# A planner that books time on TensorE for each change of product kind, with ranks and leanings chosen anew

## Chip, cores and metric

One core of a Trainium2 chip runs the whole program in one launch. The metric is device microseconds (us) of one execution; several executions are made and their median is given. The profile is of one further execution of its own.

## What is computed

The reference runs three layers after one another on float32 data (the weights of the two feed-forward layers are float64): an attention in random features, a gated feed-forward layer, and a second one with a piecewise quadratic activation.

```python
def _attn_ref(q, k, v, omega):             # 4 batches, 8 heads, 576 rows, 64 columns; omega 128 x 64
    def phi(x):
        proj = np.einsum('bhsd,md->bhsm', x, omega)
        h = proj - np.sum(x * x, axis=-1, keepdims=True) / 2.0
        h = h - np.max(h, axis=-1, keepdims=True)
        return np.exp(h) / np.sqrt(m)
    q_p, k_p = (phi(q_s), phi(k_s))
    kv = np.einsum('bhsm,bhsd->bhmd', k_p, v)
    num = np.einsum('bhsm,bhmd->bhsd', q_p, kv)
    return num / (np.einsum('bhsm,bhm->bhs', q_p, np.sum(k_p, axis=2))[..., None] + 1e-06)

def _moe_ref(x, w_gate, w_val, w_out):     # 2304 tokens, 512 -> 1536 -> 512
    g = x @ w_gate
    return g / (1.0 + np.exp(-g)) * (x @ w_val) @ w_out

def _moe2_ref(x, w_in, w_out):             # 2304 tokens, 512 -> 2048 -> 512
    h = x @ w_in
    return np.where(h >= 1, h, np.where(h <= -1, 0.0, (h + 1) ** 2 / 4)) @ w_out
```

## The kernel before

**A planner writes the order.** The kernel is a set of Python generators that yield operations (`Op`: engine, cost in us, the function that issues it), requests for buffers (`Get`) and events (`Ev`). The class `Planner` runs them in a reckoned time while the program is built; whenever it starts an operation on an engine, that instruction is issued to this engine's queue. So the planner's reckoning fixes the order of every queue (TensorE, VectorE, ScalarE, GpSimd, and SyncE for the DMAs) and, through `pick` (L264), which engine does a copy or an addition that two engines can do. On the chip each engine then goes through its queue in that order and waits where its data is not there. The costs in the plan have no other effect on the program.

**How an engine chooses.** `dispatch` (L235) takes, of what is ready for an engine, the entry with the lowest rank (`PR_...`, L62 to L67; most processes without a rank of their own have 1.0). For TensorE, `together` (L223) first narrows the list: products have kinds. `row` is a projection on omega (L654, 64x128 tiles of the array), `col` are the sums over keys (L723) and the numerators (L836; both 128x64 tiles), `turn` are transposes by the identity (L792, L846; 128x128), and `moe`, or no kind, are the feed-forward products (L418 to L420; 128x128). While feed-forward products run, attention's products are held until two of them wait or one has waited 2.0 us (`HOLD`, `HOLD_N`); after that all ready ones of one kind go first, then those of another, before the feed-forward products go on. Such a stretch of attention's products between feed-forward products is called a visit here.

**What `pick` compares.** For each engine the time at which it is free, plus the costs that wait for it, plus the operation's cost, plus `LEAN` of this engine. `LEAN["DVE"]` (VectorE) is `LEAN_A` until attention is closed and `LEAN_B` from then on (L297, L903), and `LEAN["POOL"]` (GpSimd) becomes `POOL_B` at that point. `copy` (L396) chooses between ScalarE (0.52 us for 512 elements by the planner's formula) and VectorE (0.34 from SBUF, 0.60 from PSUM); `two` (L406) between VectorE (0.60) and GpSimd (1.23). `parts` makes the two halves of a number for the three products of `split3`: a copy (the high half, L399 or L401) and a subtraction (the low half, L409 or L411).

**The stages.** Until about 50 us TensorE has attention's products alone. From there to 230 us they alternate with the first part of the first feed-forward layer (`moe1`, nine token blocks of 256, weights of the first four column groups). From 230 us on all products are feed-forward ones: `late_up`, with sets of seven products over sums and differences of blocks (`set_up`, L1343), and `late_down`. `x_make` (L1157) makes the operands of these sets on VectorE and ScalarE, `stage` and `conv_pair` convert the float64 weights on the way (`PR_ST`, `PR_W`), `front` (L634) is the first half of attention for one group of rows (`PR_FRONT` is its rank after it has its banks), and `keep_bank` (L1249) copies a PSUM bank to SBUF (`PR_BANK`).

Of the kernel before, what the change touches and what calls it, by code (L numbers as in the profile page):

```python
# [35 lines left out]
KD = 4  # L36


LEAN = {'DVE': 1.0, 'POOL': -0.38, 'ACT': -0.55}
LEAN_A, LEAN_B, POOL_B = 0.97, -0.09, 5.00  # L40
ALT = 1.63

SLACK_D, SLACK_U = 2.0, 0.8
# [15 lines left out]
N_WT, N_XU = 3, 2  # L59
N_EB, N_GB, N_HL, N_HB, N_XI = 4, 2, 2, 1, 4  # L60

PR_K, PR_Q0, PR_Q = (0.32, 0.9, 0.96, 1.0), 0.17, 1.01  # L62
PR_C0, PR_C, PR_CS = 0.66, 1.08, 0.7
PR_W = 1.06
PR_BANK = 0.3
PR_FRONT = 0.2
PR_ST, PR_X, PR_E = 1.50, 0.74, 1.45  # L67
T_V, T_Q0, T_C0 = 3.84, 2.87, 5.5
N_GATE, N_CS = 1, 3
N_WS = 2  # L70
HOLD, HOLD_N = 2.0, 2

ORDER = (0, 1, 2, 3, 4)

SETS1 = (2, 2)
SETS2 = (2, 2)
# [58 lines left out]
class Planner:  # L135
# [99 lines left out]
    def dispatch(self, eng):  # L235
        q = self.queue.get(eng)
        if not q or self.free_at.get(eng, 0.0) > self.now + 1e-9:
            return
        held = self.port > self.now + 0.02
        c = self.together(q) if eng == "PE" else q  # L240
        best = q[0] if eng in ("HW", "DMA") else min(c, key=lambda e: (held and e[2].lock, e[1].prio, e[0]))
        if held and best[2].lock:
            self.push(self.port, self.dispatch, eng)
            return
        q.remove(best)
        _, p, op = best
        self.load[eng] -= op.cost
        if op.fn is not None:
            op.fn()
        end = self.now + op.cost  # L250
        if op.lock:
            self.port = end
        if eng == "PE":
            self.kind = op.kind
            if self.now > self.free_at.get(eng, 0.0) + 0.05:
                end += 0.12
            if self.now < 4.2:
                end += op.cost
        self.free_at[eng] = end
        p.last = {eng: end}  # L260
        self.push(end, self.step, p, None)
        self.push(end + (0.001 if op.kind == "moe" else 0.0), self.dispatch, eng)

    def pick(self, **cost):  # L264

        return min(cost, key=lambda e: max(self.now, self.free_at.get(e, 0.0)) + self.load.get(e, 0.0) + cost[e]
                   + LEAN.get(e, 0.0))

# [24 lines left out]
def performer_moe_kernel(ctx: ExitStack, tc: tile.TileContext, qX, kX, vX, om, ident,  # L293
                         w1, wo1, w2, wo2, out):
    nc = tc.nc
    pl = Planner()
    LEAN["DVE"] = LEAN_A  # L297
    scale = 64.0 ** -0.25
# [298 lines left out]
    def bank_pair():  # L597

        tok = yield Get(two_banks)
        b0 = yield Get(bank)  # L600
        b1 = yield Get(bank)
        pl.put(two_banks, tok)
        return b0, b1
# [30 lines left out]
    def front(xb, n, loads, is_q, rng):  # L634
# [13 lines left out]
        rank = pl.cur.rank  # L648
        pl.cur.rank = min(pl.cur.prio, PR_FRONT)

# [169 lines left out]
    def num(k, d, q_t):  # L820
# [8 lines left out]
        banks = yield from bank_pair()  # L829
        pl.cur.rank = min(pl.cur.prio, PR_FRONT)  # L830

# [54 lines left out]
    def att_close():  # L886
# [15 lines left out]
        pl.set(right_b)  # L902
        LEAN["DVE"], LEAN["POOL"] = LEAN_B, POOL_B  # L903

# [117 lines left out]
    def part_stream():  # L1022
        yield moe1_v
        for a in range(len(SETS1)):
            for kb in ORDER:
                nt = blocks[kb][1]
# [82 lines left out]
    for m, counts, sets in ((1, SETS1, list(range(NE, NF // 2))),  # L1109
                            (2, SETS2, [(2 * q, 2 * q + 1) for q in range(NF2 // 4)])):  # L1110
        for a, n in enumerate(counts):
            passes.append((m, a, ORDER, sets[0:n]))
            sets = sets[n:]
# [16 lines left out]
    def pq(t):  # L1130
        return t.rearrange("p (k t) -> p k t", k=2)
# [114 lines left out]
    def plus(dst, ps, e):  # L1246

        yield Op("DVE", c_dve(512), lambda: nc.vector.tensor_tensor(out=dst, in0=pq(ps), in1=pq(e), op=ALU.add))  # L1248

    def keep_bank(ps, ev, into):  # L1250
        e = yield Get(ebr)
        yield from copy(e, ps, 512, False)
        into.append(e)
        pl.set(ev)
# [40 lines left out]
    def row1(key, S):  # L1295
# [4 lines left out]
        cv = pq(c22)  # L1300
        pl.cur.rank = PR_BANK
        yield from plus(cv, S["Ub"], c22)
# [40 lines left out]
    def set_up(m, a, j, c, last_s, last_x):  # L1343
# [6 lines left out]
        for bk, wk, off, u, before, then in SEVEN:  # L1350
# [24 lines left out]
            if then in ("e1", "e2", "e5"):  # L1375
                pl.spawn(keep_bank(ps, S[then], S[then + "b"]), PR_BANK)
            else:
# [77 lines left out]
    def part2_stream():  # L1455
        for a in range(len(SETS2) - 1):
            for j in ORDER:
                for c in range(blocks[j][1] // P):
# [217 lines left out]
```

## Time and profile before

| | |
|---|---|
| median of 3 runs | 929.09 us (927.48 to 931.4) |
| the profiled execution | 930.79 us |
| its span, first to last instruction | 929.0 us |
| mean granted TensorE clock | 0.999 of full speed |
| busy: TensorE, VectorE, ScalarE, GpSimd | 920.5, 774.2, 512.6, 62.4 us |

An engine is busy while one of its instructions runs. A record of a matrix product includes its way through the array (276 ns for 256 columns), while the next one starts 113 ns later; so what TensorE loses is read from the starts of its products, and from the stretches in which nothing ran.

### The profile page before, as it was taken

Reading aid. Unit: us, or ns where it says so; the run is one execution under the profiler, and the core shown is the slowest. Engines: PE = TensorE matmul, PEld = TensorE weight load, DVE = VectorE, ACT = ScalarE, POOL = GpSimd, SP = SyncE. Lnnn points to the kernel's source line nnn. Section 1 sums busy time; section 2 is a strip of 40 time slices with the busy share of each in tenths; the row PEclk is TensorE's granted clock in tenths of the full one; section 3 lists DMA queues with packets and bytes.
Section 4 is the critical chain, followed back from the end, with each engine's and each line's share of the span. In section 5 each row is a group of like instructions: output and inputs, shape, how many; then the busy total and the mean of one; then the engine's idle time right before and its main releaser. Section 6 shows DMA issues by size and latency. Waiting matters only on the chain.

```text
span 929.0 us, 22669 instructions
## 1 busy us (share of the span) xinstructions
PE 920.5 (99%) x9244; PEld 906.6 (98%) x9244; DVE 774.2 (83%) x1496; ACT 512.6 (55%) x1131; POOL 62.4 (7%) x53
## 2 busy tenths in 40 slices
PE   8999999999999999999999999999999999999998
PEld 8889999999999999999999999999999999999998
DVE  5988888865989999899989899999797679766553
ACT  7888977544445545555545466555555445434331
POOL 0213324322000000000000000000000000000000
PEclk9999999999999999999999999999999999999999
DMA  7678446555676374845476836264313131403022
GB/s 247 192 237 252 143 160 217 198 180 167 222 233 193 112 235 167 308 146 187 137 240 208 267 113 213 80 211 153 126 58 125 37 112 47 137 12 103 1 92 91
DMA packets 88665, 147.71 MB, mean 159 GB/s; under 512 B 8304, under 2 KB 43888, under 8 KB 88560
## 3 DMA queue, kind: packets, MB, share of 16 engines
q1 hardware_dynamic: 88416, 146.19, 48.3%
q8 instruction: 72, 1.18, 0.5%
q14 instruction: 33, 0.27, 0.1%
q10 hardware_dynamic: 144, 0.07, 0.0%
HBM read 103.24 MB, written 42.99 MB: 157 GB/s over the span
## 4 chain that ended last, share of the span: by engine, by line
PE 83%; DVE 7%; DMA 6%; ACT 2%; issue 1%; SPq 0%; DVEq 0%; ACTq 0%
PE bank L418 25%; PE bank L419 25%; PE bank L420 25%; PE bank L654 4%; PE bank L723 2%; PE bank L836 2%; PE bank L792 1%; DMA ws<-in_w_dram 1%; DMA ki<-in_kX_dram 1%; DMA wtr<-w32i 1%; PE bank L846 1%; DMA ws<-in_wo_dram 1%; DVE xq L411 1%; DMA wtr<-w32o 1%; DMA kl<-in_kX_dram 1%
## 5 line engine op out<-in xcount | busy, mean ns | idle before, releaser
L418 PE MATMUL bank<-x1s,w 128*128 128x256 f32 x492 | 138.0, 280 | 0.2
L420 PE MATMUL bank<-x1s,w 128*128 128x256 f32 x492 | 136.2, 277 | 0.0
L419 PE MATMUL bank<-x1s,w 128*128 128x256 f32 x492 | 136.2, 277 | 0.0
L418 PEld LDWEIGHTS bank<-x1s,w 128*128 128x128 f32 x492 | 92.5, 188 | 1.5 <-ACT qt L399 0.3
L420 PEld LDWEIGHTS bank<-x1s,w 128*128 128x128 f32 x492 | 92.5, 188 | 0.0
L419 PEld LDWEIGHTS bank<-x1s,w 128*128 128x128 f32 x492 | 92.4, 188 | 0.0
L399 ACT ACTIVATE x1s<-xq 128x512 fp32r<-128x512 f32 x84 | 52.9, 631 | 60.7 <-PE bank L420 37.8
L418 PE MATMUL bank<-x1s,wb 128*128 128x256 f32 x286 | 78.9, 276 | 0.0
L419 PE MATMUL bank<-x1s,wb 128*128 128x256 f32 x286 | 78.9, 276 | 0.0
L420 PE MATMUL bank<-x1s,wb 128*128 128x256 f32 x286 | 78.9, 276 | 0.0
L418 PE MATMUL bank<-x1s,wx 128*128 128x256 f32 x278 | 77.4, 278 | 0.4 <-ACT eb L399 0.4
L419 PE MATMUL bank<-x1s,wx 128*128 128x256 f32 x278 | 76.8, 276 | 0.0
L420 PE MATMUL bank<-x1s,wx 128*128 128x256 f32 x278 | 76.8, 276 | 0.0
L435 ACT ACTIVATE wt<-ws 128x512 f32<-128x512 f32 x68 | 46.3, 684 | 46.7 <-DMA ws<-in_w_dram 23.4
L399 ACT ACTIVATE eb<-bank 128x512 f32<-128x512 f32 x96 | 56.6, 590 | 25.4 <-PE bank L420 25.1
L411 DVE TENSOR_TENSOR x1s<-xq,x1s 128x512 fp32r<-128x512 f32 x90 | 62.4, 694 | 7.5 <-ACT x1s L399 7.4
L663 DVE TENSOR_REDUCE st<-bank 128x4 f32<-128x512 f32 (+1 forms) x76 | 48.0, 659 | 17.1 <-PE bank L654 17.0
L1248 DVE TENSOR_TENSOR gb<-bank,eb 128x512 f32<-128x512 f32 x64 | 44.4, 693 | 12.7 <-PE bank L420 12.5
L419 PEld LDWEIGHTS bank<-x1s,wb 128*128 128x128 f32 x286 | 53.7, 188 | 0.0
L420 PEld LDWEIGHTS bank<-x1s,wb 128*128 128x128 f32 x286 | 53.7, 188 | 0.0
L418 PEld LDWEIGHTS bank<-x1s,wb 128*128 128x128 f32 x286 | 53.7, 188 | 0.0
L418 PEld LDWEIGHTS bank<-x1s,wx 128*128 128x128 f32 x278 | 52.2, 188 | 1.1 <-ACT eb L399 0.6
(253 smaller groups left out, 3322.6 us busy)
## 6 DMA issues: line engine op xcount, KB each, us to landing
ws<-in_w_dram SPq DMA_DIRECT2D x40, 512.0 KB, 4.7
ws<-in_wo_dram SPq DMA_DIRECT2D x28, 512.0 KB, 5.3
xq<-x1d SPq DMA_DIRECT2D x36, 256.0 KB, 4.7
xq<-x2d SPq DMA_DIRECT2D x36, 256.0 KB, 4.0
qi<-in_qX_dram SPq DMA_DIRECT2D x28, 256.0 KB, 4.2
ki<-in_kX_dram SPq DMA_DIRECT2D x22, 256.0 KB, 4.7
x1d<-os SPq DMA_DIRECT2D x18, 256.0 KB, 4.7
op<-os SPq DMA_DIRECT2D x18, 256.0 KB, 2.8
```

What stands on the lines that cost most here:

```text
L399: yield Op("ACT", c_act(n), lambda: nc.scalar.activation(dst, src, AF.Copy, scale=1.0 if scale is None else scale))
L411: yield Op("DVE", c_dve(n), lambda: nc.vector.tensor_tensor(out=dst, in0=a, in1=b, op=op), True)
L418: nc.tensor.matmul(ps, l_hi, r_hi, start=first, stop=False, skip_group_check=shared)
L419: nc.tensor.matmul(ps, l_hi, r_lo, start=False, stop=False, skip_group_check=shared)
L420: nc.tensor.matmul(ps, l_lo, r_hi, start=False, stop=last, skip_group_check=shared)
L435: yield Op("ACT", 0.575, lambda: nc.scalar.activation(t, hw.bitcast(F32), AF.Abs))
L654: nc.tensor.matmul(banks[a][:, u * P:(u + 1) * P], xb[h, l, u * P:(u + 1) * P], r[h], start=first and (last or u == 0), stop=last, skip_gr ...
L663: yield Op("DVE", c_dve(256 * n), lambda: nc.vector.tensor_reduce(out=sv[:, a, units, 3 if by_pe else 0], in_=pv[a], axis=AX.X, op=ALU.max ...
L723: nc.tensor.matmul(kp[h, 2 * pr + a, 0:65], es[:, a, u * P + 64 * m:u * P + 64 * m + 64], v[:, 65 * a:65 * a + 65], start=(li == 0 and a = ...
L792: nc.tensor.transpose(tp[:, (a * 2 + t) * P:(a * 2 + t + 1) * P], es[:, a, u * P:(u + 1) * P], ids)
L836: nc.tensor.matmul(banks[t][rows, 65 * h:65 * h + 65], q_t[:, h // 2, h % 2, t * P + 64 * m:t * P + 64 * m + 64], kvr[tiles[t][m], d][:, h ...
L1248: yield Op("DVE", c_dve(512), lambda: nc.vector.tensor_tensor(out=dst, in0=pq(ps), in1=pq(e), op=ALU.add))
```

## The change

The class `Planner` gets a table `SWITCH`, and `dispatch` adds time to a TensorE operation that is not of the kind of the one before it: nothing from `turn` to a feed-forward product or to no kind, 0.12 us from these to `turn`, 0.2 us for every other change; from `moe` to no kind and back nothing. Besides, some of the leanings and ranks have new values. No process, buffer or instruction of the kernel is edited.

```diff
-LEAN = {'DVE': 1.0, 'POOL': -0.38, 'ACT': -0.55}
-LEAN_A, LEAN_B, POOL_B = 0.97, -0.09, 5.00
+LEAN = {'DVE': 1.0, 'POOL': -0.586, 'ACT': -0.322}
+LEAN_A, LEAN_B, POOL_B = 0.823, -0.524, 5.0
...
-PR_K, PR_Q0, PR_Q = (0.32, 0.9, 0.96, 1.0), 0.17, 1.01
-PR_C0, PR_C, PR_CS = 0.66, 1.08, 0.7
+PR_K, PR_Q0, PR_Q = (0.32, 0.9, 0.96, 1.082), 0.17, 1.129
+PR_C0, PR_C, PR_CS = 0.68, 1.234, 0.7
 PR_W = 1.06
-PR_BANK = 0.3
-PR_FRONT = 0.2
-PR_ST, PR_X, PR_E = 1.50, 0.74, 1.45
+PR_BANK = 0.194
+PR_FRONT = 0.33
+PR_ST, PR_X, PR_E = 1.5, 0.491, 1.45
...
+SWITCH = {("turn", "moe"): 0.0, ("turn", None): 0.0, ("moe", "turn"): 0.12, (None, "turn"): 0.12}
...
         if eng == "PE":
+            if op.kind != self.kind and not (self.kind in ("moe", None) and op.kind in ("moe", None)):
+                end += SWITCH.get((self.kind, op.kind), 0.2)
             self.kind = op.kind
```

## Rows read from the trace of the kernel before

**Rows 1.** The page: busy time of each engine, and the granted clock by slices.

```profile
PE 920.5 (99%) x9244; PEld 906.6 (98%) x9244; DVE 774.2 (83%) x1496; ACT 512.6 (55%) x1131; POOL 62.4 (7%) x53
...
PEclk9999999999999999999999999999999999999999
```

**Rows 2.** Stages: stretch, length, busy us (instructions) by engine, clock, DMA share, GB/s.

```profile
12.00:54.00 42.00, 40.64 (x770) 37.00 (x766) 39.13 (x81) 37.23 (x111) 9.13 (x7) 1.00 0.71 226
54.00:230.00 176.00, 175.27 (x2255) 167.69 (x2254) 140.66 (x323) 121.58 (x374) 51.51 (x39) 1.00 0.58 188
230.00:300.00 70.00, 70.00 (x614) 69.61 (x613) 63.22 (x119) 36.37 (x65) 1.29 (x1) 1.00 0.68 224
300.00:650.00 350.00, 348.88 (x3066) 347.88 (x3066) 334.32 (x634) 189.85 (x354) 0.00 (x0) 1.00 0.57 184
650.00:925.00 275.00, 275.00 (x2429) 275.00 (x2429) 193.16 (x336) 120.68 (x215) 0.00 (x0) 1.00 0.24 78
```

**Rows 3.** TensorE's waits, whole span: waiting line, releaser, total us, times, longest.

```profile
PE bank L418 <- ACT eb L399: 1.0, 2, 0.6
PE bank L846 <- DVE os L401: 0.7, 1, 0.7
...
PE bank L654 <- ACT os L399: 0.7, 1, 0.7
```

**Rows 4.** The chain that ended last, its end: start, length, engine, line.

```profile
925.26 0.13 PE bank L420
...
925.41 0.42 DVE os L1512
```

**Rows 5.** TensorE's timeline around three visits (start, length, line, tiles, count).

```profile
72.66 0.28 PE L420 MATMUL bank<-x1s,w 128*128 128x256 f32 x1
72.87 1.16 PE L654 MATMUL bank<-omr,ki 64*128 64x128 f32 x16
73.96 0.38 PE L418 MATMUL bank<-x1s,w 128*128 128x256 f32 x1
...
112.57 0.28 PE L420 MATMUL bank<-x1s,w 128*128 128x256 f32 x1
112.69 1.04 PE L792 MATMUL bank<-ids,ebq 128*128 128x128 f32 x8
113.48 0.36 PE L418 MATMUL bank<-x1s,wx 128*128 128x256 f32 x1
...
222.59 0.28 PE L420 MATMUL bank<-hl,w 128*128 128x256 f32 x1
222.80 2.09 PE L836 MATMUL bank<-kvr,qt 128*64 128x65 f32 x64
224.82 0.38 PE L418 MATMUL bank<-hl,w 128*128 128x256 f32 x1
```

**Rows 6.** The chain in the first 230 us: pieces of one kind, short and long.

```profile
18.91 1.09 PE bank L654 x16
20.00 0.59 PE bank L792 x4
31.86 1.99 PE bank L654 x32
33.84 1.08 PE bank L836 x32
...
156.34 2.02 PE bank L836 x64
```

**Rows 7.** Copies, 300 to 650 us: L399 on ScalarE, L401 on VectorE; one form of L401.

```profile
300.00:650.00 350.00, 127.44 (x223) 1.00 0.57 184
300.00:650.00 350.00, 5.12 (x12) 1.00 0.57 184
L401 DVE CAST xur<-xq x7: 418/427/430, 322.2 to 826.6; 128x512 fp32r<-128x512 f32 x7
```

**Rows 8.** GpSimd's subtraction L409, its first 230 us (shortest/median/longest ns).

```profile
L409 POOL TENSOR_TENSOR x1s<-os,x1s x14: 1282/1346/1882, 42.6 to 212.3; 128x512 fp32r<-128x512 f32 x14
```

## Prediction, made before the changed kernel was run

> **What bounds the kernel now.** The page comes first. TensorE is busy for 920.5 of 929.0 us, and its granted clock is at the upper of its two levels (2.4 GHz) in every slice [rows 1], so neither more clock nor a large hole is to be had. The table by stages says where the missing 8.5 us lie: 1.36 between 12 and 54 us, 0.73 between 54 and 230, nothing from 230 to 300, 1.12 between 300 and 650, nothing from 650 to 925 [rows 2]; the rest is the first 12 us and the end. After the last product only a sum of 0.42 us and the end of the program follow [rows 4]; the change reaches neither. Third, TensorE's waits: the longest sum is 1.0 us in two waits, the others shown are 0.7 each, and that view has six rows in all [rows 3]. So the kernel is TensorE's list of products, one after another, and the program after the change has the same products. Only three things can move the time: what is lost between products of different kinds, TensorE's few waits (1.36 + 0.73 + 1.12 = 3.2 us between 12 and 925 us), and new waits.
>
> The same table shows what could become late: VectorE is busy 334.32 of 350 us between 300 and 650 us, while ScalarE is busy 189.85 [rows 2].
>
> **What a change of kind costs on the chip.** I take it from starts, not from lengths. A feed-forward product starts 0.113 us after the last (350 us hold 3066 of them [rows 2], 0.114 with the waits). A visit with 16 `row` products: last feed-forward start 72.66, next one 73.96, so 1.30 less 0.11 is 1.19 us [rows 5]. Sixteen such products cost 1.99 - 1.09 = 0.90 us in a longer piece [rows 6]; the two changes of kind cost 0.29. A visit with 64 `col` products: 224.82 - 222.59 - 0.11 = 2.12 [rows 5]; 32 of them cost 2.02 - 1.08 = 0.94 [rows 6], 64 so 1.88, and the two changes 0.24. A visit with eight transposes: 113.48 - 112.57 - 0.11 = 0.80 [rows 5]; two pieces of four that stand between other kinds cost 2 x 0.59 = 1.18 [rows 6], so changes from feed-forward products to transposes and back cost nothing that the rows show. A change into or out of `row` or `col` thus costs 0.12 to 0.15 us.
>
> **What the new reckoning books.** The code books 0.446 x 2 + 0.1 = 0.99 us for the `row` visit; measured is 1.19; the change books 0.4 more, 1.39. Two numerators are 2.04 in the code, measured 2.12, after the change 2.44. Eight transposes are 0.88, measured 0.80, afterwards 1.00. So the switch term goes the right way for `row` and then past the mark by as much as it fell short, and past it for the other two, since the constants in the costs (0.1 here, 0.15 at L726) already held most of it. Along the timeline from 12 to 230 us I count 114 changes of kind (25 visits from 54 us on, three of which are shown [rows 5]; 16 changes from `turn` to feed-forward, 8 back): 90 x 0.2 + 8 x 0.12 = 19 us booked, against 90 x 0.12 to 0.15, or 11 to 13 us, that the chip takes, a good part of which was booked before.
>
> The Trainium skill, in "TensorEngine Tiling (Array Packing)", section "Key Properties", says that changing the tiling mode, not just the tile, drains TensorE. The visit of transposes, which have the feed-forward products' full tile, agrees: no loss [rows 5]. By that rule the 0.12 from feed-forward to `turn` books a drain that isn't there; it is 1 of the 19 us.
>
> **The change part by part.** (1) *The switch term.* It adds no instruction and no wait. It only makes a plan in which a visit lasts longer: 0.4 us on a mean visit of 3.05 us (my sum over the 25 is 76 us), an eighth. In that time more of attention's products become ready, and `together` takes them along. If an eighth fewer changes follow, 114 becomes 100 and 14 x 0.12 = 1.7 us go. Bounds: 0, and half of them, 57 x 0.12 = 6.8 us. I take 1.7, as the mechanism is that small and the hold rule itself (two products or 2.0 us) is untouched.
>
> (2) *Ranks.* `PR_Q` and the last of `PR_K` fall behind weight conversion (1.06) and behind elementwise work at 1.0; `PR_FRONT` falls behind the first batch's 0.32; `PR_BANK` and `PR_X` move without passing any rank that meets them on VectorE or ScalarE. On SyncE's queue `PR_X` = 0.491 puts the operand loads before part loads (0.5) and weight loads (0.6). All this only reorders queues in front of TensorE, which has work in 175.27 of 176 us while attention lasts [rows 2]. I take 0, with one or two waits of the size seen, 0.7 us [rows 3], to either side. What hides it is the stock of ready feed-forward products; without it, attention's own latency would show, as in the 1.36 us between 12 and 54 us [rows 2].
>
> (3) *Leanings until 230 us.* VectorE's handicap against ScalarE falls from 0.97 + 0.55 = 1.52 to 0.823 + 0.322 = 1.145, and rises against GpSimd from 1.35 to 1.41. A few copies go to VectorE (busy 140.66 of 176) from ScalarE (121.58) [rows 2], a subtraction or two to GpSimd, where one takes 1.35 us [rows 8]. Both engines have room: 0.
>
> (4) *Leanings after 230 us.* This is the larger edit. For a copy from SBUF, ScalarE was taken if its backlog was below VectorE's plus 0.27 us (0.336 - 0.09 - 0.523 + 0.55); now only if it is below VectorE's less 0.39. Between 300 and 650 us ScalarE does 223 copies at L399, from SBUF and from PSUM, VectorE 12 at L401 [rows 7]. A copy is 0.42 us of VectorE's time [rows 7] at the most, and VectorE has 350 - 334.32 = 15.7 us free [rows 2]: room for 37 copies. Because the comparison counts VectorE's backlog, copies move mainly into its holes. I take 20 moved copies, 8.4 us, wholly in free time, so 0 on the path; the bounds are a gain of the 1.12 us of waits of that stretch, both counted waits being for a ScalarE copy [rows 3], and the loss of the rival below.
>
> Sum: 929.0 - 1.7 = 927.3 us of span. The profiled run lay 1.79 us above its span and 1.70 above the median of the runs, so 927.3 + 1.79 - 1.70 = 927.4 us.
>
> **The rivals.** *A: the plan becomes really better.* If half of the changes of kind go (6.8 us) or, more likely, a quarter (3.4), and most of the 3.2 us of waits, it is 929.1 - 3.4 - 2.6 = 923. For: every avoidable loss lies in what the new constants touch. Against: all there is between the kernel and its floor is 6.8 + 3.2 = 10 us, and the visits grow little.
>
> *B: VectorE fills up (slower).* The price begins when more than 37 copies move in 300 to 650 us: then VectorE is the bound of that stage, and every further one costs 0.42 us. Sixty moved copies give 23 x 0.42 = 9.7 us: 939. For: VectorE is 96% busy there and ScalarE's copies are 223 in number [rows 2, 7]. Against: a full VectorE has a backlog, and the comparison then still chooses ScalarE.
>
> *C: the book is too slow (slower).* In the plan TensorE is late by up to 19 us of bookings, so the plan lets other engines take their time; on the chip TensorE arrives earlier and waits. With ten waits of 0.7 us [rows 3] it is 936. For: the measured visits lie below the new booking in all three cases. Against: the engines run as early as their data allows, whatever was booked.
>
> The Trainium skill, "SBUF — State Buffer", section "Who interferes with whom", says that VectorE's two-port copies and GpSimd's work exclude each other for a whole instruction. GpSimd's subtractions reach 1.88 us where 1.28 is the shortest [rows 8], which fits; copies moved to VectorE before 230 us would stretch some by 0.6 us, which adds to C and not to the sum.
>
> *D: nothing.* The term reorders, the losses stay: 929.1.
>
> **How the numbers follow.** Forecast 0.37, D 0.20, A 0.20, B 0.11, C 0.12. About 0.5% (4.6 us) is what a measurement of this kernel can tell from no change. Forecast and D are within it, A lies over it (923 is 6 below), B and C lie over it on the other side: faster 0.20, same 0.57, slower 0.23. The range goes from 921.5, where A has taken three quarters of its 10 us, to 937, which takes in C and the lighter half of B.
>
> **What would show it.** Right: fewer changes of kind before 230 us and the same 0.12 to 0.15 for each; attention's products unchanged in number; TensorE's waits still around 3 us; in 300 to 650 us some tens of copies at L401 instead of 12. For A: the stretch to 230 us shorter by 4 us or more. For B: TensorE's share below 99% between 300 and 650 us, waiting for VectorE. For C: new waits before 230 us. Wrong would be a gain or a loss after 650 us, where TensorE never waits [rows 2].

## The result, and the profile after

The changed kernel takes 935.95 us (median of 5 runs, 934.02 to 937.91) against 929.09 (median of 5, 927.48 to 931.4); the ratio, of means, is 1.0066 with a 95% interval of 1.0041 to 1.0092. It is slower by some 6 us. The profiled execution took 936.34 us, its span is 934.5, so 5.5 us above that of before, and its clock was at the upper level throughout.

The table by stages of the changed kernel has the columns of [rows 2].

```profile
12.00:54.00 42.00, 39.26 (x736) 35.65 (x736) 41.18 (x78) 35.89 (x110) 9.44 (x7) 1.00 0.71 220
54.00:230.00 176.00, 170.97 (x2252) 163.80 (x2246) 148.69 (x340) 121.95 (x366) 52.08 (x40) 1.00 0.65 209
230.00:300.00 70.00, 70.00 (x618) 70.00 (x619) 64.54 (x127) 30.04 (x53) 2.10 (x2) 1.00 0.67 230
300.00:650.00 350.00, 347.82 (x3056) 346.99 (x3056) 336.40 (x649) 170.60 (x320) 0.00 (x0) 1.00 0.53 172
650.00:925.00 275.00, 275.00 (x2428) 275.00 (x2427) 221.62 (x406) 86.03 (x154) 0.00 (x0) 1.00 0.24 78
```

TensorE stands idle 2.74 us between 12 and 54 us (1.36 before) and 5.03 between 54 and 230 (0.73 before): 7.77 against 2.09. Between 300 and 650 us it is 2.18 against 1.12. After 650 us nothing is lost, as before.

TensorE's waits of the changed kernel, with the columns of [rows 3]: four new ones of 1 to 2 us, two of them for VectorE, two for ScalarE.

```profile
PE bank L657 <- DVE ki L634: 2.1, 1, 2.1
PE bank L795 <- DVE rec L817: 2.0, 1, 2.0
PE bank L421 <- ACT eb L402: 1.6, 2, 0.8
PE bank L726 <- ACT ebk L687: 1.5, 1, 1.5
...
PE bank L795 <- ACT qt L402: 1.0, 1, 1.0
```

(The line numbers of the changed kernel are larger by 3.) The page's summary of the chain that ended last: TensorE carries 68% of it and VectorE 20%, against 83% and 7% on the page of before (second line).

```profile
PE 68%; DVE 20%; DMA 7%; ACT 2%; issue 2%; SPq 1%; DVEq 0%; ACTq 0%
...
PE 83%; DVE 7%; DMA 6%; ACT 2%; issue 1%; SPq 0%; DVEq 0%; ACTq 0%
```

From 50 to 100 us the chain runs almost wholly through VectorE. Its busy time in that stretch (columns of [rows 2]) is 49.73 of 50 us in the changed kernel, where it was 44.98 before (second line):

```profile
50.00:100.00 50.00, 48.04 (x825) 44.96 (x822) 49.73 (x121) 45.45 (x191) 15.60 (x11) 1.00 0.76 239
...
50.00:100.00 50.00, 49.33 (x810) 45.48 (x809) 44.98 (x113) 42.85 (x161) 13.06 (x10) 1.00 0.73 230
```

**Two of the waits in the timeline** of the changed kernel (start, length, engine, line, what it writes and reads; in brackets how long the engine stood idle before it, and for whom):

```profile
44.07 0.41 DVE L441 TENSOR_SCALAR wt<-wt 128x512 uint32<-128x512 uint32 x1
44.22 1.39 POOL L412 TENSOR_TENSOR w<-wt,w 128x512 fp32r<-128x512 f32 x1 [4.03 <-DVE w L404]
44.40 1.75 DVE L634 SCALAR_TENSOR_TENSOR ki<-ki 128x512 f32<-128x512 f32 x1
46.21 1.05 PE L657 MATMUL bank<-neg,ki 64*128 64x128 f32 x14 [2.13 <-DVE ki L634]
...
120.95 1.53 PE L795 MATMUL bank<-ids,ebq 128*128 128x128 f32 x12
122.03 0.67 ACT L438 ACTIVATE wt<-ws 128x512 f32<-128x512 f32 x1 [1.75 <-DMA ws<-in_w_dram]
122.73 0.43 DVE L439 TENSOR_SCALAR wt<-wt 128x512 f32<-128x512 f32 x1 [1.14 <-ACT wt L438]
123.19 0.43 DVE L441 TENSOR_SCALAR wt<-wt 128x512 uint32<-128x512 uint32 x1
124.03 0.42 DVE L817 TENSOR_TENSOR rec<-bank,st 128x256 f32<-128x256 f32 x1
124.50 0.66 PE L795 MATMUL bank<-ids,ebq 128*128 128x128 f32 x4 [2.02 <-DVE rec L817]
```

In the first, VectorE comes from steps of a weight conversion (L441) to the squares that TensorE needs, and these run beside a subtraction on GpSimd and take 1.75 us. In the second, TensorE needs a bank that L817 has to empty; L817 stands in VectorE's queue behind a weight conversion, that conversion waits for its step on ScalarE, and ScalarE waits for the weights' DMA. In this second wait VectorE and ScalarE both stood idle just before, so no engine is short of time; a queue is held up by work that attention has no need of.

**What the change did save.** Counted along TensorE's timeline, 114 changes of kind became 91, and 25 visits 18.

**The books.** Idle time before 230 us +5.7, between 300 and 650 us +1.1, 23 fewer changes at 0.12 us -2.8: +4.0 of the 5.5 us. The other 1.5 us don't show as idle time. They lie in gaps shorter than what a product's record covers (276 ns, with the next start after 113). If every product and change of kind is given the price that it has in visits without waits, the starts are later than that by 2.9 us more than before between 12 and 54 us, and by 4.5 us more from there to the end of attention; less the 2.5 us of the changes saved, at these prices, and with 0.7 us in the rest, that is 5.6, the difference between the starts of the last products.

### The profile page after: what moved, and what is told of

Read it like the earlier page. It is cut to its first block, busy times and chain, and to the rows that moved or that the text cites. A ratio compares the mean times of both kernels' runs of the same rounds, so it can differ in the third digit from the quotient of the medians.

```text
span 934.5 us, 22633 instructions
## 1 busy us (share of the span) xinstructions
PE 919.5 (98%) x9244; PEld 906.5 (97%) x9244; DVE 817.2 (87%) x1605; ACT 451.0 (48%) x1013; POOL 64.1 (7%) x54
## 4 chain that ended last, share of the span: by engine, by line
PE 68%; DVE 20%; DMA 7%; ACT 2%; issue 2%; SPq 1%; DVEq 0%; ACTq 0%
PE bank L421 21%; PE bank L422 21%; PE bank L423 21%; DVE st L666 3%; DMA xq<-x1d 2%; DMA ws<-in_w_dram 2%; DVE wt L443 1%; PE bank L657 1%; SPq L395 1%; DVE wt L445 1%; PE bank L839 1%; DVE ebk L683 1%; DVE x1s L414 1%; DVE xq L414 1%; DVE wt L439 1%
## 5 line engine op out<-in xcount | busy, mean ns | idle before, releaser
L402 ACT ACTIVATE eb<-bank 128x512 f32<-128x512 f32 x81 | 47.9, 592 | 37.7 <-PE bank L423 36.4
L402 ACT ACTIVATE x1s<-xq 128x512 fp32r<-128x512 f32 x58 | 36.5, 629 | 41.0 <-DVE xq L414 18.4
```

Source lines behind the costliest of these rows:

```text
L402: yield Op("ACT", c_act(n), lambda: nc.scalar.activation(dst, src, AF.Copy, scale=1.0 if scale is None else scale))
```

## Experiments

All comparisons are with the kernel before on the same chip (medians 929.1 to 930.0 us there). The booking is the new term in `dispatch`; "constants" are the new ranks and leanings together.

**The booking and the constants apart.** Two theories. *The book*: the booking makes the plan's TensorE slower than the chip's; the other queues are filled to that pace, with other work in front of what attention needs, and on the chip TensorE waits. *The leanings* (B of the prediction): VectorE got too much work. First the constants without the booking:

```diff
-                end += SWITCH.get((self.kind, op.kind), 0.2)
+                end += SWITCH.get((self.kind, op.kind), 0.0)
-SWITCH = {("turn", "moe"): 0.0, ...}
+SWITCH = {}
```

(The old table is shortened here.)

> The changed kernel without the booking (SWITCH empty, nothing added), with its new ranks and leanings. Theory C (the booking makes the plan slower than the chip's TensorE, the other queues are filled to that slower pace, and TensorE waits for them before 230 us): TensorE's idle time between 12 and 230 us goes back from 7.8 us to 2 to 3, time 928 to 931 us. Theory B (the leanings fill VectorE): VectorE's busy time stays near 817 us and the waits stay, 934 to 937 us. Theory R (the ranks put attention behind weight conversion): the same 934 to 937 us.

Measured: 932.0 us, ratio 1.0023 (1.0014 to 1.0033). VectorE's busy time from 12 to 925 us is 812.8 us, as much as with the change (812.4), and yet 4 of the 6 us are gone. TensorE's idle time before 230 us is 4.0 us: between the two theories, and both it and the time are a little over what theory C gave.

Then the booking on the kernel before:

```diff
+SWITCH = {("turn", "moe"): 0.0, ("turn", None): 0.0, ("moe", "turn"): 0.12, (None, "turn"): 0.12}
...
         if eng == "PE":
+            if op.kind != self.kind and not (self.kind in ("moe", None) and op.kind in ("moe", None)):
+                end += SWITCH.get((self.kind, op.kind), 0.2)
```

> The kernel before with the booking of the change (0.2 us, 0.12 and 0), old ranks and leanings. Theory C: 933 to 940 us, most of the loss as idle time of TensorE before 230 us, and fewer changes of kind than 114. Theories B and R: 927 to 931 us, as none of their edits is in it.

Measured: 935.52 us, ratio 1.0064 (1.0052 to 1.0076), idle time before 230 us 6.6 us, and 99 changes of kind. The booking alone gives the whole of the loss.

**Half of it, twice of it**, with the new constants:

```diff
-                end += SWITCH.get((self.kind, op.kind), 0.2)
+                end += SWITCH.get((self.kind, op.kind), 0.1)     # 0.4 in the other; 0.12 becomes 0.06, 0.24
```

> The changed kernel with half the booking (0.1 us for a change of kind, 0.06 into transposes). Theory C: between the constants alone and the change, 929 to 933 us. Theories B and R: no different from the change, 934 to 937 us.

Measured: 929.19 us, ratio 1.0001 (0.9990 to 1.0011). The range of theory C holds, but not its order: this is 2.8 us less than the constants alone, which book nothing (932.0).

> The changed kernel with twice the booking (0.4 us, 0.24 into transposes). Theory C: TensorE waits more than in the change, 940 to 955 us, the loss before 240 us. Theories B and R: 933 to 938 us, a little less by the changes of kind that are saved.

Measured: 949.39 us, ratio 1.021 (1.0196 to 1.0223). Its stages before 230 us:

```profile
12.00:54.00 42.00, 37.75 (x645) 34.08 (x642) 39.45 (x78) 34.98 (x95) 9.11 (x7) 0.96 0.65 207
54.00:230.00 176.00, 166.48 (x2192) 156.40 (x2191) 146.68 (x334) 119.39 (x341) 43.92 (x34) 0.99 0.65 210
```

TensorE idles 13.8 us there. Its granted clock is 0.96 in the first of the two stretches and 0.99 in the second: for a part of each it was at the lower of its two levels (1.2 GHz), after waits of 1.9 and 2.7 us, and that is some 1.7 us of each. VectorE has less to do in both stretches than in the change (39.45 and 146.68 us against 41.18 and 148.69), and the longest waits are for ScalarE:

```profile
PE bank L795 <- ACT os L402: 2.7, 1, 2.7
PE bank L421 <- ACT ebk L679: 2.5, 2, 1.6
PE bank L849 <- ACT ebq L679: 1.9, 1, 1.9
```

Yet there are fewer changes of kind than in any other kernel with these constants (89, and 91 with the full booking). Saving them is not what decides.

**Is it the amount of VectorE's work?** The same plan and the same order, with less in VectorE's queue:

```diff
-        yield Op("DVE", c_dve(512), lambda: nc.vector.scalar_tensor_tensor(
+        yield Op("DVE", c_dve(512), lambda: pl.now > 225.0 and nc.vector.scalar_tensor_tensor(
             out=ti, in0=lw, scalar=29, ...
```

and the same for the step after it.

> The changed kernel, same plan and same order, but the last two of the four VectorE steps of each weight conversion before the plan's 225 us are left out (some 31 conversions, 62 instructions of 0.60 us, 37 us of VectorE's queue), so the weights lack their sign and low bits. Theory C1 (the plan filled VectorE's queue to the booked pace, and on the chip that queue is the bound of 50 to 140 us): most of the added loss goes, 925 to 930 us, and TensorE's idle time from 12 to 230 us falls from 7.8 to below 4 us. Theory C2 (the waits come from the order alone, ScalarE's and the DMAs' times among it, not from the amount of VectorE's work): less than 2 us of change, 934 to 937 us.

Measured: 929.94 us, ratio 1.001 (0.9997 to 1.0022), so 6 us less than the change. The stages of it:

```profile
12.00:54.00 42.00, 39.95 (x766) 36.77 (x763) 36.57 (x75) 38.94 (x122) 9.93 (x8) 1.00 0.75 241
54.00:230.00 176.00, 172.56 (x2248) 165.85 (x2247) 118.29 (x293) 119.52 (x355) 48.96 (x40) 1.00 0.63 209
...
300.00:650.00 350.00, 349.56 (x3076) 348.98 (x3075) 338.55 (x653) 169.76 (x316) 0.00 (x0) 1.00 0.53 174
```

VectorE has 30 us less to do between 54 and 230 us, and TensorE still idles 5.5 us before 230 us, of 7.8. The time came out as theory C1 had it, the idle time did not (below 4 was expected). Both waits shown above are still there, 1.5 and 1.4 us long:

```profile
PE bank L657 <- DVE ki L634: 1.5, 1, 1.5
PE bank L795 <- DVE rec L817: 1.4, 1, 1.4
```

Of the 6.1 us by which the span got shorter (934.5 to 928.4), 1.7 are idle time between 300 and 650 us (0.44 against 2.18), where no step was left out. So at most some 4.4 us come from the stretch in which VectorE had less to do.

> The kernel before with the same steps left out. Theory C1: little to gain, since TensorE was the bound already, 926 to 929 us. Theory C2: the same as before, 928 to 931 us. If VectorE had been the bound of that stretch already before the change: below 924 us.

Measured: 929.46 us, ratio 1.0004 (0.9992 to 1.0016): nothing, though VectorE's work fell as much. (It is inside C2's range and just above C1's, so this run by itself doesn't choose between them.)

```profile
54.00:230.00 176.00, 176.00 (x2273) 169.10 (x2273) 111.06 (x281) 122.94 (x379) 48.52 (x40) 1.00 0.59 195
```

So taking VectorE's work out speeds up the changed kernel and not the one before. But the idle time that stayed says that the amount is a part of it only; the rest is where things stand in the queues, as in the second wait above.

**A book that agrees with the trace.** The prices of a change of kind are those of the visits without waits in both traces, and the constants in the operations' costs go:

```diff
+SWITCH = {frozenset(k): v for k, v in ((("row", "moe"), 0.155), (("col", "moe"), 0.125), (("turn", "moe"), 0.0),
+                                       (("row", "col"), 0.175), (("row", "turn"), 0.174), (("col", "turn"), 0.135))}
...
+            end += SWITCH.get(frozenset((self.kind or "moe", op.kind or "moe")), 0.0)
...
-        yield Op("PE", 0.446 * n + 0.1, lambda: proj(0, omr, True, not by_pe), kind="row")
+        yield Op("PE", 0.446 * n, lambda: proj(0, omr, True, not by_pe), kind="row")
... (the same for the second projection)
-        yield Op("PE", 0.232 * len(todo) + 0.15, mm, kind="col")
+        yield Op("PE", 0.234 * len(todo), mm, kind="col")
...
-        yield Op("PE", 1.02, mm, kind="col")
+        yield Op("PE", 0.938, mm, kind="col")
...
-        yield Op("PE", 0.55, trans, kind="turn")
+        yield Op("PE", 0.44, trans, kind="turn")
```

> The kernel before with TensorE's costs booked as the trace shows them: 0.155 us for row to or from feed-forward, 0.125 for col, 0 for turn, 0.175 row to col, 0.174 row to turn, 0.135 col to turn, and the constants in the costs of the operations (0.1, 0.15, 0.08, 0.11) taken out. Old ranks and leanings. If the loss comes from booking the switches on top of those constants, this one is near before: 926 to 931 us. If any booking of changes does harm by itself: 933 to 937 us.

Measured: 930.14 us, ratio 1.0015 (1.0002 to 1.0029): near the kernel before.

> The same measured booking with the ranks and leanings of the change. If the loss comes from booking the switches on top of the constants: 928 to 932 us, as with half the booking. If the ranks and leanings need the full booking to work: 933 us or more.

Measured: 929.24 us, ratio 0.9998 (0.9986 to 1.0010). It has the same leanings and ranks as the change, and TensorE hardly waits in attention any more:

```profile
12.00:54.00 42.00, 41.97 (x781) 37.67 (x780) 40.77 (x82) 37.10 (x112) 9.03 (x7) 1.00 0.73 220
54.00:230.00 176.00, 175.82 (x2267) 168.51 (x2267) 145.59 (x338) 118.01 (x366) 52.66 (x42) 1.00 0.59 195
```

Between 54 and 230 us VectorE has 145.59 us of work here and 148.69 in the change: nearly the same amount, in another order, and 0.2 us of waits instead of 5.0.

**Leanings and ranks apart**, without booking. Each is the kernel before with some of the new constants:

```diff
-LEAN = {'DVE': 1.0, 'POOL': -0.38, 'ACT': -0.55}
-LEAN_A, LEAN_B, POOL_B = 0.97, -0.09, 5.00
+LEAN = {'DVE': 1.0, 'POOL': -0.586, 'ACT': -0.322}
+LEAN_A, LEAN_B, POOL_B = 0.823, -0.524, 5.0
```

in the one, and in the other

```diff
-PR_K, PR_Q0, PR_Q = (0.32, 0.9, 0.96, 1.0), 0.17, 1.01
+PR_K, PR_Q0, PR_Q = (0.32, 0.9, 0.96, 1.082), 0.17, 1.129
```

with the other `PR_` lines of the change.

> The kernel before with the new leanings alone (no booking, old ranks). VectorE's busy time goes up by some 40 us as in the change. If the leanings are free, as the prediction put it: 928 to 930.5 us and no more waits than before. If they make the 2.5 us by which the constants alone were slower: 931 to 933 us, with waits between 12 and 54 us.

Measured: 927.95 us, ratio 0.9981 (0.9973 to 0.9990): the leanings gain about 1.8 us. This is the one kernel that beats both.

> The kernel before with the new ranks alone (no booking, old leanings). If the 2.5 us of the constants come from the ranks (the first batch's products ahead of other groups' fronts, attention behind weight conversion): 931 to 933 us, with waits between 12 and 54 us. If the ranks are free: 928 to 930.5 us.

Measured: 931.29 us, ratio 1.0021 (1.0012 to 1.0030), idle time before 230 us 4.1 instead of 2.1. The ranks alone lose as much as all the constants together (1.0023). But the leanings alone gain nearly as much, so the two do not add up.

**All four sets of constants at each booking.** These kernels put together the edits that are shown above. Half the booking with the old constants, then with the leanings:

> The kernel before with half the booking (0.1 and 0.06 us), old ranks and leanings. If the amount booked sets the loss and not the constants: 928 to 931 us, between the kernel before and the booking alone (935.5 us). If half a booking was harmless only with the new ranks and leanings: 932 us or more.

Measured: 930.49 us, ratio 1.0009 (1.0000 to 1.0019). VectorE does the last step (L445) of 7 weight conversions between 12 and 54 us here, and of 5 between 54 and 90:

```profile
12.00:54.00 42.00, 4.25 (x7) 1.00 0.72 225
54.00:90.00 36.00, 3.21 (x5) 1.00 0.75 240
```

> The kernel before with the new leanings and half the booking (0.1 and 0.06 us), old ranks. If the parts add up (leanings -1.5 us, half a booking 0 to +1 us): 927.5 to 929.5 us. If the saved changes of kind come on top, as with half the booking and all new constants: 925 to 927 us. If it is 930 us or more, the parts don't add up, and what one of them brings depends on the whole order.

Measured: 937.28 us, ratio 1.0082 (1.0069 to 1.0094). This miss, too, says that the parts do not add up. Its waits are spread: 3.1 us before 230 us, and 4.6 between 230 and 650. The longest in its timeline:

```profile
357.73 0.66 ACT L438 ACTIVATE wt<-ws 128x512 f32<-128x512 f32 x1 [2.66 <-DMA ws<-in_wo_dram]
358.29 0.61 ACT L402 ACTIVATE x1s<-xq 128x512 fp32r<-128x512 f32 x1
358.81 0.58 ACT L402 ACTIVATE eb<-bank 128x512 f32<-128x512 f32 x1
...
359.44 0.39 PE L421 MATMUL bank<-xur,w 128*128 128x256 f32 x1 [2.00 <-ACT eb L402]
```

The copy of a bank that TensorE needs is third in ScalarE's queue, behind a weight conversion that waits 2.66 us for its DMA. It is the second wait of the changed kernel again, on another engine, and after the last product for which the booking adds anything.

So one plan's loss could be its own. The table was completed to tell the booking from that: the full booking with the leanings and with the ranks, half of it with the ranks, twice of it with the old constants.

> Full booking with the new leanings, old ranks. If the amount booked sets the loss: 932 to 939 us, at least 4 us over the leanings alone (928.0), the loss before 240 us. If each order of the queues has a loss of its own that the booking only reshuffles: anywhere from 928 to 938 us.

Measured: 936.93 us, ratio 1.0072 (1.0053 to 1.0092).

> Full booking with the new ranks, old leanings. If the amount booked sets the loss: 933 to 940 us, over the ranks alone (931.3), the loss before 240 us. If each order has a loss of its own: anywhere from 928 to 938 us.

Measured: 939.78 us, ratio 1.0094 (1.0074 to 1.0114).

> Half the booking with the new ranks, old leanings: the fourth plan at half. If the amount booked sets the loss: 930 to 934 us. If each order has a loss of its own, half a booking may give as much as 938 us again, as it did with the leanings.

Measured: 930.62 us, ratio 1.0007 (0.9993 to 1.0021).

> The kernel before with twice the booking (0.4 and 0.24 us), old ranks and leanings. If the amount booked sets the loss: 943 to 955 us as with the new constants (949.4), the loss before 250 us. If each order has a loss of its own: 930 to 940 us.

Measured: 945.57 us, ratio 1.0164 (1.0142 to 1.0186).

And the measured booking with the other two sets:

> The measured booking (changes at 0.125 to 0.175 us, constants taken out) with the new leanings and old ranks. If waits before 230 us follow how far the book lies from the chip: TensorE idle from 12 to 230 us at most 1.5 us, as with the other two plans at this booking (1.0 and 0.2), against 1.9 for the leanings without booking and 3.1 with half of it. If each order has a wait of its own: anything up to 4 us. In time: 927 to 931 us if nothing is lost after attention.

Measured: 932.0 us, ratio 1.0033 (1.0019 to 1.0047), idle time before 230 us 3.5 us: not as expected.

> The measured booking with the new ranks and old leanings. If waits before 230 us follow how far the book lies from the chip: TensorE idle from 12 to 230 us at most 1.5 us, against 4.1 for the ranks without booking and 7.2 with all of it. If each order has a wait of its own: anything up to 4 us. In time: 928 to 932 us.

Measured: 933.43 us, ratio 1.0048 (1.0033 to 1.0062), over the expected range. Idle before 230 us it is 0.9, as expected; but 2.8 us between 300 and 650 us, where most is for ScalarE's copies of banks.

Median time, and TensorE's idle time from 12 to 230 us (218 us less its busy time there, read from one execution each), in us:

| booking | old constants | leanings | ranks | both |
|---|---|---|---|---|
| none | 929.09, 2.1 (before) | 927.95, 1.9 | 931.29, 4.1 | 932.0, 4.0 |
| measured | 930.14, 1.0 | 932.0, 3.5 | 933.43, 0.9 | 929.24, 0.2 |
| half | 930.49, 1.3 | 937.28, 3.1 | 930.62, 2.5 | 929.19, 2.9 |
| full | 935.52, 6.6 | 936.93, 5.3 | 939.78, 7.2 | 935.95, 7.8 (the change) |
| twice | 945.57, 8.2 | | | 949.39, 13.8 |

The four plans with the full booking lie over all four without (935.5 to 939.8 against 928.0 to 932.0), whatever the constants, and both at twice over these. That is the amount booked. Within a row the order of the queues moves the time by 4 us, and at half by 8; in the rows up to half the booking can't be told from the order. The accurate book has the smallest waits before 230 us with three of the four sets, but a better time than no booking with one only (both, 929.24 against 932.0).

The amount of VectorE's work does not set the idle time by itself. From 12 to 230 us it is 190.30 us in the measured booking with the leanings (first line) and 189.87 in the change, with 3.5 and 7.8 us of idle time:

```profile
12.00:230.00 218.00, 214.50 (x3025) 203.87 (x3022) 190.30 (x418) 152.83 (x470) 56.38 (x44) 1.00 0.62 197
...
12.00:230.00 218.00, 210.23 (x2980) 199.45 (x2978) 189.87 (x417) 157.84 (x474) 61.52 (x47) 1.00 0.66 211
```

## Why the prediction was wrong

The forecast was 927.4 us, a gain of 1.7; it became a loss of 6.9 between the medians. The time lies where rival C put it (936).

**What bounds the kernel.** Right: the products are the same 9244 in number, and nothing moved after 650 us. Only before 230 us and between 300 and 650 us did waits change. One reading was off, without effect on the sum: the longest of the six waits of the kernel before is 1.2 us, not 1.0; it lies in the first 12 us.

```profile
PE bank L1583 <- DVE hb L1581: 1.2, 1, 1.2
```

**The price of a change of kind.** Right, as far as it went. Between feed-forward products and `row` or `col` it is 0.155 and 0.125 us; between two of attention's kinds 0.135 to 0.175. With these prices, with minus 0.04 us between transposes and feed-forward products, and with 0.0558, 0.0293 and 0.109 us for a `row`, `col` and `turn` record, 30 of the 32 visits without waits in both traces come out within 0.03 us (the other two within 0.08). So transposes still cost nothing to enter.

**What the booking books.** Right, and the key to the result: it was worked out that the new reckoning goes past the measured visits in all three cases [rows 5, 6]. The experiments at full and twice the booking bear that out; half books 1.19, 2.24 and 0.94 us for the three visits, nearer to the measured 1.19, 2.12 and 0.80, and three of the four sets lose nothing by it that is clear of the order's 4 us.

**Term (1), the changes saved.** The saving was right in mechanism and size: the booking alone takes 114 to 99, 15 fewer where 14 were forecast. The change has 23 fewer, or 2.8 us at 0.12 each; the constants alone take away 7 (107 are left). What the term left out is the waits that the booking brings.

**The step that failed** is in term (1), that the booking adds no wait, and in what gave C a chance of 0.12: that the engines run as early as their data allows, whatever was booked. The booking alone took TensorE's idle time before 230 us from 2.1 to 6.6 us and lost 0.64%, all of the change's loss. In the waits followed here, each engine runs its queue in order, and in the plan with a slower TensorE other work stands in front of what attention needs. Between 12 and 90 us VectorE does the last step of 6 + 5 weight conversions in the changed kernel (the stages of that line, L445), and 5 + 3 before:

```profile
12.00:54.00 42.00, 4.07 (x6) 1.00 0.71 220
54.00:90.00 36.00, 3.41 (x5) 1.00 0.77 247
...
12.00:54.00 42.00, 3.43 (x5) 1.00 0.71 226
54.00:90.00 36.00, 2.06 (x3) 1.00 0.76 238
```

Their number alone does not make the loss: half the booking with the old constants has 7 and 5 there, and idles 1.3 us. What seems to count is which step stands in front of which, and that was followed for single waits only.

In the change VectorE was busy 49.73 of 50 us between 50 and 100 us, and at 122 us, where it was not, it waited with a conversion whose DMA had landed late. The cover named in (2), the stock of ready feed-forward products behind TensorE's 175.27 us of work in 176 [rows 2], was a property of the old order and went with it: 170.97. C's direction was right; that its 936 was hit to the microsecond is luck, as ten waits of 0.7 us were a guess, and the trace has a few of 1 to 2 us and many short gaps.

**Term (2), the ranks**, taken as 0 with a wait or two of 0.7 us to either side: alone they lose 0.2% (1.9 us), a little outside.

**Terms (3) and (4), the leanings**, taken as 0: alone they gain 0.2%. Copies moved as estimated. Between 300 and 650 us VectorE does 44 copies instead of 12, and ScalarE 192 instead of 223 [rows 7]:

```profile
300.00:650.00 350.00, 110.51 (x192) 1.00 0.53 172
...
300.00:650.00 350.00, 19.90 (x44) 1.00 0.53 172
```

That is 32 more, where 20 were assumed and there was room for 37. A copy is not 0.42 us at the most: the 44 take 19.90 us, 0.45 each, as six of them are from PSUM at 0.68. VectorE's busy time rose from 334.3 to 336.4 us only, and with the leanings alone TensorE idles 1.11 us in that stretch, as before (1.12). So rival B fell. Where the leanings' gain of 1.8 us comes from was not settled.

**The Trainium skill's rule on tiling modes** ("TensorEngine Tiling (Array Packing)", "Key Properties") held: the full-tile transposes go in and out of the feed-forward products at no cost that the trace shows. The Trainium skill's rule on the shared port ("SBUF — State Buffer", "Who interferes with whom") was put down as something that adds to C, and the trace agrees, though not for a two-port copy: the squares at L634 are an instruction with two SBUF inputs, which that section names too, beside a GpSimd instruction that reads SBUF. They took 1.75 us there and 0.69 without it.

**What stays open.** How the 6 us divide between the amount of VectorE's work and the order of the queues: taking work out gave back all of the time, but only 2.3 of the 5.7 us of idle time before 230 us, and 1.7 us after 300, where nothing was taken out; and with twice the booking the longest waits are for ScalarE. That the order of the queues makes the waits is shown for the single ones above and argued for the rest. Why half the booking with all the constants is faster than none stays open too. And why half the booking with the leanings alone loses 7 us: one wait of it is shown above, the rest was not followed.

## What to carry to other kernels

A cost that a planner books is not only a forecast, it decides what is put in front of what. Booking time that the chip does not take can do more harm than leaving the term out: here 0.2 us for each change of kind lost 6 us, and no booking at all lost nothing against the measured prices in three sets of four. Before adding a term, look whether a constant in the operations' costs already holds it, and compare the sum with a whole visit in the trace. And where any change reorders every queue, one plan's time carries a chance of some 4 us here, in one row 8: judge such a term at several doses and with several sets of the other constants before believing a sign.

## What the runs showed of the hardware

- A VectorE instruction with both operands in SBUF took 1.75 us beside a GpSimd subtraction of 1.39 us, where one of the same line and shape took 0.69 us without it. TensorE's wait of 2.13 us ended with it.
- A weights' DMA of 512 KB landed after 4.7 us in the median (68 in the changed kernel), and the one that was waited for at 122 us after 6.2. The planner reckons 3.85 us from its issue to the first use when no other transfer is before it: 1.59 for the bytes (L394), the rest in fixed steps (`dma` and `LAT`). At 122 us the late landing reached TensorE because the waiting conversion stood in front of L817 in VectorE's queue.
- Entering or leaving 64-row or 64-column tiles costs TensorE 0.125 to 0.175 us each time, by the fit to 32 visits; transposes on the full tile between feed-forward products cost none.
